# A planned order of some 3,600 steps, planned again with later transfers: fused block-sparse attention and a gated MLP on one core

## The chip, the core and the metric

The kernel runs on one core of a Trainium2 chip. Its work is spread over TensorE (PE, with its weight loads shown apart as PEld), VectorE (DVE), ScalarE (ACT), GpSimd (POOL) and the DMA queue that SyncE (SP) feeds; each of them carries out its own instructions in the order in which they were written and waits at semaphores for the others. The metric is the device time of one execution in microseconds (us), lower is better. Three runs of the kernel before took 992.58, 995.05 and 990.33 us; their median is 992.58 us.

## What is computed

The reference is attention with a block mask, followed by an MLP whose middle is `h * relu6(h + 3) / 6`:

```python
batch, n_heads, seq, head_dim = (4, 8, 768, 64)
scores = scale * np.matmul(q, k.transpose(0, 1, 3, 2))
...
scores = np.where(mask, scores, -1000000000.0)
scores = scores - np.max(scores, axis=-1, keepdims=True)
attn = np.exp(scores)
attn = attn / (np.sum(attn, axis=-1, keepdims=True) + 1e-09)
x = np.matmul(attn, v)          # then heads side by side: 3072 x 512
h = x @ w_in                    # 512 -> 2048
g = h * np.clip(h + 3.0, 0.0, 6.0) / 6.0
out = g @ w_out                 # 2048 -> 512
```

All inputs are float32. The mask works on blocks of 32 keys: neighbours, first and last block, and three sampled blocks in each row.

## The kernel before

**Two kinds of work, 64 pieces each.** A *unit* (`u0` to `u63`) is one head, one batch and half of the queries (384). A *step* (`m0` to `m63`) is one eighth of the MLP (two 128-wide chunks of the hidden layer) for one half batch. The MLP is computed with each fp32 number split into a high part and a low part, so a step has three products where one would do: high by high, high by low, low by high. The split of the two weight matrices is made by 32 pieces of *weight* work (`w0` to `w31`) in the first 210 us or so: load, four to five DVE and ACT passes, and a store of the low half to DRAM (`save`), from which steps load it again (`loadin_0`, `loadin_1`, `loadout_0`, `loadout_1`; tiles `wlo_in` and `wlo_out`, four buffers each). The high halves stay in SBUF (`win_hi`, `wout_hi`).

**A unit's steps.** `loadq`, `loadk`, `loadv` bring `qraw`, `kraw` and `vo` (one buffer of `qraw` and of `kraw`). `qh` and `kh` (ACT) and `ql` (DVE) make the tiles `QA` and `KA`; `kl` (POOL) and `qb` (ACT) make the low parts `kb` and `qb`. `m_0` to `m_2` (PE) compute scores whose block maxima `r_0` to `r_2` (DVE, tile `bm`) take; `fin_0`, `fin_1` give the row maximum `mneg`; `mt` carries it into a row of `qb` (from unit 10 on by a small DMA). `s_0` to `s_2` (PE) compute the scores again with the maximum and the mask added, `e_0` to `e_2` (ACT) the exponentials `pr`, `suma` to `sumc` (DVE) the sums, `av` (PE) the product with the values. `tt` (ACT) and `uu` (DVE) bring the product out of PSUM. For four units together `dm` (PE), `dc` (ACT), `rg` (four small DMAs), `rc` (DVE), `rs` and `rb` (DMAs by way of DRAM) make the reciprocal of the sums; `ux_0`, `ux_1`, `ux_2` (DVE, ACT, DVE) multiply by it and split the result into the pair `xhl`, which the steps read.

**A step's.** `h_00` to `h_11` (six matmuls each of 384 columns) fill one PSUM tile `big`; `ga` (ACT), `gb` (DVE), `gh` (ACT), `gl` (POOL) make `ghi` and `glo`; `o_00` to `o_21` (three matmuls each of 512 columns) add into `out0` to `out2`. The low halves of the weights are read by the third matmul of each three in `h` and by the second in `o`. Every eighth step ends with `oc` (DVE copies) and `od` (stores).

**What sets the order.** Nothing is scheduled at run time. The table `SCORE` (lines 41 to 299) lists some 3,600 steps in one order; `play` (line 858) goes through it and emits the instructions of each, and the wrapper `Ordered` (line 325) pins every instruction to that program order on its engine. The tile library adds the semaphores. The table was written by a planner from assumed durations and landing times. PSUM has two `big` tiles, one `av` tile and three `out` tiles. All work goes through the wrapper's line, so the profile names L333 nearly everywhere; tiles tell the steps apart.

Of the kernel before, what the change touches and what calls it, by code (L numbers as in the profile page):

```python
# [46 lines left out]
    bits_1; u2 qh; u0 e_1 av_1 e_2; u2 ql; w1 bits_2; u1 r_1 kl; w1 high low; u0 av_2; u1 m_2 r_2 fin_0 fin_1; u0 uc;
    u2 loadk kh m_0; w5 load; w3 size; u1 mt; u2 kl r_0; u3 loadk; u1 qm s_0 s_1; w3 bits_0; u2 m_1; w5 size bits_0;
    u1 e_0; u0 dw; w5 bits_1; u1 s_2; w3 bits_1; u1 e_1; w5 bits_2 high; u1 av_0; u2 loadv; u1 e_2; u2 qb; u3 loadq
    qh; u2 r_1 m_2; u1 av_1 av_2; u3 qb; w0 save; w5 low; u2 r_2 fin_0; w3 bits_2; u3 kh; u2 fin_1 mt; w3 high; u3 ql  # L50
    m_0 r_0; w4 load; u3 kl; w6 load; u2 qm s_0; w4 size; u3 m_1; u2 e_0; u1 uc; u2 s_1; u1 dw; w4 bits_0; u3 r_1; u2
    e_1 s_2; u3 m_2; w4 bits_1 bits_2; u4 loadq qh loadk; w6 size; u1 rg; u4 kh; u2 av_0; u3 r_2; u4 ql; w6 bits_0;
    u2 av_1 e_2; u3 fin_0; u4 qb; u3 fin_1; u1 rc; u4 m_0 r_0; u3 mt qm loadv; u2 av_2; w6 bits_1; w4 high low; u2
    uc; u3 s_0 e_0; u5 loadq; u2 dw; w6 bits_2 high; u4 m_1 r_1 kl; w3 low; u3 s_1 s_2; w7 load; u4 m_2 r_2; u5 qh ql
    loadk; u3 e_1; u1 rs; w8 load; u4 fin_0; u5 kh; w6 low; u6 loadq; u3 av_0; u4 fin_1; u3 av_1; u5 m_0 r_0; u4 mt;
    u3 e_2; w7 size; w8 size; u5 kl; w8 bits_0; u3 av_2; u4 qm s_0; w7 bits_0; u1 rb; w8 bits_1; u4 loadv; u5 m_1
    r_1; u4 s_1; u3 dw; u6 loadk; u4 e_0; w8 bits_2; u3 uc; w7 bits_1; u1 ux_0; u3 rg; u4 s_2 e_1; w10 load; u6 qh ql
    kh; u5 m_2 r_2; u4 e_2 av_0 av_1; u6 m_0; u3 rc; u4 av_2; u1 ux_1; u6 kl; u7 loadq; u5 qb; w8 high; w10 size; u7
    loadk; u5 loadv; w6 save; u5 fin_0 fin_1 mt; u6 r_0; w7 bits_2; u6 m_1; w10 bits_0; u6 r_1; u5 qm; u6 loadv; u4
    uc; w7 high low; w4 save; u5 s_0 s_1; u6 m_2; u5 e_0; u4 dw; u5 s_2 e_1 av_0 av_1; u1 ux_2; w10 bits_1; u6 r_2;  # L60
    w2 save; u7 qh ql; w9 load; u3 rs; u6 fin_0; w10 bits_2; u5 e_2; u6 fin_1; u7 kh m_0 r_0; u6 qb; w9 size; u6 mt;
    u7 kl; u6 qm; u5 av_2; u8 loadq; w8 low; w10 high low; u5 dw; w9 bits_0; u6 s_0 e_0; u7 m_1 r_1; m1 loadin_0; w9
    bits_1; u5 uc; u6 s_1 e_1; u3 rb ux_0; w9 bits_2; u6 s_2; w3 save; u8 loadk; u7 m_2; u8 qh ql kh; u6 av_0 av_1
    e_2; u5 rg rc; u7 r_2 fin_0; w11 load; w12 load; u8 kl; u3 ux_1 ux_2; w11 size; u7 fin_1; u6 av_2; w11 bits_0; w5
    save; w10 save; u8 m_0; u7 qb; u8 r_0; u7 mt; w9 high; u6 uc; w11 bits_1; u7 qm; w9 low; u7 s_0; u6 dw; u7 e_0;
    u8 m_1 r_1; u5 rs; w12 size bits_0; u7 s_1 e_1; w8 save; u7 s_2 loadv; u8 m_2; u9 loadk kh loadq; u7 av_0; u9 kl;
    u7 e_2; u9 qh; u7 av_1; m1 loadout_0; w7 save; u7 av_2; u5 rb; u8 qb; m0 loadout_1; u9 qb; w11 bits_2; w12
    bits_1; w14 load; u8 r_2 fin_0; u5 ux_0; u8 fin_1; u9 ql; w11 high low; u10 loadk; u5 ux_1; u8 mt qm; u9 m_0 m_1
    r_0; u7 dw uc; u10 loadq; w14 size; u8 s_0; u9 r_1; u8 e_0 s_1 s_2 e_1; w9 save; u10 kh kl; w12 bits_2 high; u10
    qh; m1 loadin_1; u8 loadv; m0 loadout_0; w14 bits_0 bits_1 bits_2; u9 m_2; u5 ux_2; u7 rg rc; u8 av_0; u9 r_2; u8  # L70
    av_1 e_2; u9 fin_0 fin_1 mt; w16 load size; u8 av_2; w14 high; u10 ql m_0; w16 bits_0 bits_1; u9 loadv; m1
    loadout_1; u9 qm; w18 load; u7 rs; u8 uc dw; u10 r_0; u9 s_0 e_0; w14 low; w16 bits_2; w18 size; u11 loadk; u9
    s_1 e_1; u10 qb; w11 save; u7 rb; w18 bits_0; u9 s_2 e_2 av_0; u11 kh; w18 bits_1 bits_2; w12 low; u10 m_1 r_1
    m_2 r_2; m0 loadin_1; u9 av_1; m0 loadin_0; w18 high; u7 ux_0; u10 fin_0; w16 high; u11 loadq; w13 load; w14
    save; u11 qh ql; u7 ux_1 ux_2; w1 save; w12 save; m0 h_00; w13 size bits_0 bits_1; w15 load size; w13 bits_2; m0
    h_10; w17 load; u12 loadq; m0 h_01; u9 av_2 dw; u11 qb; m0 h_11 ga; u11 kl loadv; w15 bits_0 bits_1; u10 fin_1
    mt; w15 bits_2; w16 low save; m1 h_00; m0 gb; m1 h_10 h_01 h_11; w18 low; u10 qm s_0; w13 high; u12 loadk; w19
    load; w15 high; m0 gh gl; w18 save; m2 loadin_0; w17 size; w13 low save; m0 o_00 o_10 o_20; m1 ga; u9 rg; u10
    loadv e_0; w17 bits_0; u9 uc; w15 low; u10 s_1; w19 size; w17 bits_1; m1 gb; u10 e_1 s_2; u12 kh; u10 e_2; m0
    o_01; w17 bits_2; w19 bits_0; u11 m_0; w22 load; w15 save; m2 loadin_1; u12 qh kl; m0 o_11 o_21; w19 bits_1  # L80
    bits_2; m1 gh; u11 r_0; w20 load; u11 m_1 m_2 r_1 r_2 fin_0; w22 size; w19 high; w20 size; u10 av_0; u12 ql; w17
    high; w19 low; u11 fin_1; w22 bits_0 bits_1; m1 gl; w22 bits_2; m2 h_00 h_10 h_01 h_11; u12 m_0; m2 ga; w20
    bits_0; m1 o_00 o_01; w17 low; w20 bits_1; u12 r_0; w22 high; u12 qb; m2 gb; m1 o_10; w19 save; u11 mt qm; m2 gh
    loadout_1; u12 m_1; m1 o_11; w20 bits_2; u12 m_2; m1 o_20; u12 r_1 r_2 fin_0; w21 load size bits_0 bits_1; w20
    high; u10 av_1; u12 fin_1; u11 s_0; w21 bits_2; u11 s_1; u13 loadk; u11 e_0; u13 loadq; w24 load; w22 low; m2
    loadout_0; w17 save; u11 e_1; m1 o_21; u11 s_2; w24 size; u13 qh; w21 high; u10 av_2 dw; m3 loadout_0; w24
    bits_0; m2 gl o_00 o_10; u12 mt; m3 loadin_1; u12 qm; w23 load; w22 save; u11 e_2; u12 s_0 s_1; m2 o_01; u10 uc;
    u9 rc; m3 loadout_1; m2 o_11; w24 bits_1 bits_2; u13 kh; u11 av_0; u12 e_0; w21 low; w23 size; w24 high; w20 low;
    u13 ql m_0; w21 save; u12 loadv; w23 bits_0 bits_1; w24 low; u13 r_0 kl; w26 load size; u9 rs; u12 e_1; m2 o_20;
    m3 loadin_0; w23 bits_2; u11 av_1; w23 high; m4 loadin_0; u9 rb; u13 m_1 m_2; u11 av_2; w26 bits_0; u13 r_1 r_2;  # L90
    w20 save; u14 loadq; u12 s_2; u11 dw; w26 bits_1 bits_2; u11 uc; u13 fin_0; w23 low; u9 ux_0; w26 high; m3 h_00
    h_01 h_10; u12 e_2; w24 save; u12 suma; u14 qh; w25 load; u14 loadk kh kl; m5 loadin_0; u14 qb; u13 qb fin_1; m3
    h_11; u14 ql m_0; w28 load; u14 r_0; m3 ga gb gh; u12 sumb; w28 size; u12 av; u14 m_1; m4 loadin_1; u11 rg; u13
    mt qm; u14 r_1; u13 s_0; m3 gl; u13 e_0; m2 o_21; u14 m_2; u15 loadk; m3 o_00; m4 loadout_0; u13 s_1; u11 rc; u14
    r_2; u13 s_2; u12 tt; w25 size; m3 o_01; u13 e_1 e_2; w25 bits_0 bits_1; m4 h_00 h_10; m5 loadin_1; u15 loadq;
    u13 loadv; m4 h_01; u15 qh; w26 low; w25 bits_2 high; u14 fin_0; u12 sumc; w25 low; u15 ql; m4 loadout_1; u15 kh
# [809 lines left out]
```

## Time and profile before

| | before |
|---|---|
| three runs, median | 992.58 us (990.33 to 995.05) |
| the profiled execution's own time | 991.15 us |
| its span, first to last instruction | 989.4 us |
| PE busy / weight loads busy | 947.2 us / 769.7 us |
| DVE, ACT, POOL busy | 620.6, 465.3, 247.4 us |
| DMA | 155 MB, 737 issues, all from SP |

The span is the length of the profiled execution between its first and its last instruction; 1.75 us of its own time lie outside. Matmul rows overlap: a 384-column matmul is listed with 338 ns, while the next one begins some 175 ns later. A stretch's own pace is therefore read from rows of many matmuls in the chain of waits (so many matmuls in so many us), and idle time from what stands in brackets behind a row: how long the engine stood still before it and what ended that.

### The profile page before, as it was taken

The page shows a single profiled execution, that of the slowest core. Times are in us where ns is not written, and L with a number is a line of the kernel's source. Part 1 is how long each engine was busy: PE and PEld are TensorE (multiplying, and loading weights), DVE is VectorE, ACT ScalarE, POOL GpSimd, SP SyncE. Part 2 cuts the span into 40 slices and gives each one's busy share as a digit, 9 for nine tenths or more (in the row PEclk, how much of TensorE's full clock was granted, in tenths as well). Part 3 has the DMA queues.
Part 4 walks back from the last instruction along what each step waited for, and adds up shares of the span by engine and source line. Part 5 has one row for each costly group of instructions (what it writes and reads, how often), then busy time and mean ns, then how long its engine had stood idle before and what let it go on. Part 6 is the DMA issues. An engine that isn't in the chain of part 4 may idle for free.

```text
span 989.4 us, 13166 instructions
## 1 busy us (share of the span) xinstructions
PE 947.2 (96%) x4756; PEld 769.7 (78%) x4756; DVE 620.6 (63%) x924; ACT 465.3 (47%) x712; POOL 247.4 (25%) x148
## 2 busy tenths in 40 slices
PE   5998999999999999999999999999999999999998
PEld 4665787877787788877877788897788778888997
DVE  6988887955757555487565576676655686543111
ACT  5888765543444344435454444354353544442211
POOL 3222222221313122223232322132322222222122
PEclk9999999999999999999999999999999999999999
DMA  5679876664254443544435446346434444353533
GB/s 179 194 227 272 264 266 218 200 196 136 86 171 133 155 155 118 155 144 132 149 124 163 127 128 206 104 128 185 146 108 152 148 139 132 115 157 99 163 107 106
DMA packets 103700, 155.47 MB, mean 157 GB/s; under 512 B 32819, under 2 KB 51891, under 8 KB 103636
## 3 DMA queue, kind: packets, MB, share of 16 engines
q1 hardware_dynamic: 103636, 154.64, 50.0%
q8 instruction: 37, 0.61, 0.3%
q14 instruction: 27, 0.22, 0.1%
HBM read 139.63 MB, written 14.78 MB: 156 GB/s over the span
## 4 chain that ended last, share of the span: by engine, by line
PE 71%; DMA 14%; DVE 7%; ACT 3%; SPq 3%; issue 2%; DVEq 0%; ACTq 0%
PE big L333 39%; PE out L333 21%; PE av L333 11%; SPq L333 3%; DMA kraw<-kT 3%; DMA qb<-mneg 2%; DVE bm L333 2%; DVE xhl L333 2%; DMA wout_lo<-xhl 2%; DMA rec<-rec 1%; DMA wraw<-w_out 1%; DMA wlo_in<-win_lo 1%; DMA win_lo<-xhl 1%; ACT pr L333 1%; DVE acc L333 1%
## 5 line engine op out<-in xcount | busy, mean ns | idle before, releaser
L333 PE MATMUL big<-xhl,win_hi 128*128 128x384 f32 x1024 | 263.3, 338 | 0.3 <-DVE bm L333 0.2
L333 DVE TENSOR_REDUCE bm<-big 128x24 f32<-128x768 f32 x168 | 158.4, 953 | 105.6 <-PE big L333 104.7
L333 POOL TENSOR_TENSOR glo<-g,ghi 128x768 fp32r<-128x768 f32 x64 | 120.6, 1885 | 389.4 <-ACT ghi L333 380.1
L333 ACT ACTIVATE pr<-big 128x768 f32<-128x768 f32 x192 | 152.8, 810 | 125.5 <-PE big L333 123.0
L333 POOL TENSOR_TENSOR kb<-kraw,KA 64x768 fp32r<-64x768 f32 x64 | 122.0, 1907 | 340.3 <-ACT KA L333 267.0
L333 PEld LDWEIGHTS big<-xhl,win_hi 128*128 128x128 f32 x1024 | 186.0, 188 | 10.6 <-issue 3.7
L333 PE MATMUL big<-xhl,wlo_in 128*128 128x384 f32 x512 | 173.2, 338 | 2.4 <-DMA wlo_in<-win_lo 2.4
L333 PE MATMUL av<-pr,vo 128*64 128x384 f32 (+1 forms) x768 | 164.7, 497 | 1.3 <-DVE uu L333 0.6
L333 PE MATMUL out<-wlo_out,ghi 128*128 128x512 f32 x384 | 151.4, 394 | 3.1 <-DMA wlo_out<-wout_lo 3.1
L333 PE MATMUL out<-wout_hi,glo 128*128 128x512 f32 x384 | 152.9, 398 | 0.3 <-POOL glo L333 0.3
L333 PE MATMUL out<-wout_hi,ghi 128*128 128x512 f32 x384 | 153.1, 399 | 0.0
L333 PE MATMUL big<-QA,KA 128*128 128x384 f32 x384 | 136.8, 356 | 2.8 <-DVE g L333 1.1
L333 PE MATMUL big<-qb,kb 97*128 97x384 f32 x384 | 133.6, 348 | 5.3 <-DMA qb<-mneg 2.5
L333 PEld LDWEIGHTS av<-pr,vo 128*64 128x64 f32 (+1 forms) x768 | 66.9, 147 | 67.6 <-issue 48.8
L333 ACT ACTIVATE g<-big,half_b 128x768 f32<-128x768 f32 x64 | 57.7, 902 | 126.1 <-PE big L333 111.7
L333 DVE SCALAR_TENSOR_TENSOR g<-g,big 128x768 f32<-128x768 f32 x64 | 60.8, 950 | 82.9 <-ACT g L333 82.6
L333 PE MATMUL big<-KA,QA 128*128 128x384 f32 x336 | 93.5, 369 | 16.9 <-ACT KA L333 11.3
L333 PEld LDWEIGHTS big<-KA,QA 128*128 128x128 f32 x336 | 75.0, 255 | 41.1 <-ACT KA L333 13.5
L333 PEld LDWEIGHTS big<-xhl,wlo_in 128*128 128x128 f32 x512 | 96.1, 188 | 3.1 <-DMA wlo_in<-win_lo 3.1
L333 PEld LDWEIGHTS big<-QA,KA 128*128 128x128 f32 x384 | 74.0, 193 | 17.8 <-issue 3.0
L333 ACT CAST ghi<-g 128x768 fp32r<-128x768 f32 x64 | 53.2, 832 | 71.0 <-PE out L333 44.7
L333 PEld LDWEIGHTS out<-wout_hi,glo 128*128 128x128 f32 x384 | 72.4, 188 | 18.1 <-POOL glo L333 0.7
(63 smaller groups left out, 937.4 us busy)
## 6 DMA issues: line engine op xcount, KB each, us to landing
wlo_in<-win_lo SPq DMA_DIRECT2D x126, 256.0 KB, 3.6
wlo_out<-wout_lo SPq DMA_DIRECT2D x126, 256.0 KB, 3.5
kraw<-kT SPq DMA_DIRECT2D x64, 384.0 KB, 3.7
qraw<-qT SPq DMA_DIRECT2D x64, 192.0 KB, 2.8
vo<-vP SPq DMA_DIRECT2D x64, 192.0 KB, 3.6
wraw<-w_in SPq DMA_DIRECT2D x16, 512.0 KB, 4.2
wraw<-w_out SPq DMA_DIRECT2D x16, 512.0 KB, 3.6
rec<-rec SPq DMA_DIRECT2D x64, 96.0 KB, 3.1
```

Of the source, the lines that this page charges most:

```text
L333: return lambda *a, **k: tc.keep_in_program_order(op(*a, **k))
```

## The change

Everything outside the table `SCORE` stays word for word. The table has the same steps, each once, in another order. The planner that wrote it was told later landing times for transfers and longer times for issuing them. Two lines of it, before and after:

```diff
-    u0 loadq qh; k0 samp; u0 loadk; k0 table; u0 ql kh m_0; k0 index; u0 m_1; k0 ind allow_0; w0 load size; k0 kb_0
...
-    o_00 loadout_1 o_01 o_10 o_11 oc_0 od_0 oc_1 od_1 o_20 o_21 oc_2 od_2"""
...
+    m_0 r_0; m41 o_10; m43 h_00; u53 m_1; u54 qh; m43 loadin_1 h_10; u53 r_1; u54 ql; m43 h_01; u52 suma; u54 m_0;
...
+    oc_2 od_2 od_1"""
```

**Place one, the DMA queue of SP around the load of step `m5`'s second output chunk.** `wout_lo11` is that chunk in DRAM, `wlo_out` the tile it lands in, `spread<-rec` the four small DMAs of unit 15's `rg`. Before:

```order
L333 DMA wlo_out_2016<-wout_lo10_100 128x512
L333 DMA spread_2044<-rec_2026 32x1x12 x4
L333 DMA vo0_119<-vP 128x384
L333 DMA wout_lo13_103<-xhl_1790 128x512
L333 DMA wlo_out_2084<-wout_lo11_101 128x512
L333 DMA wlo_in_2091<-win_lo3_77 128x512
L333 DMA rec15_2106<-spread_2044 128x12
```

And in the changed kernel:

```order
L333 DMA wout_lo12_102<-xhl_1650 128x512
L333 DMA win_lo15_89<-xhl_1867 128x512
L333 DMA wlo_out_1991<-wout_lo11_101 128x512
L333 DMA wlo_in_2013<-win_lo14_88 128x512
L333 DMA wraw_2016<-w_out 128x1024
L333 DMA wlo_in_2037<-win_lo15_89 128x512
L333 DMA wlo_in_2040<-win_lo0_74 128x512
L333 DMA kraw_2042<-kT 128x768
L333 DMA wlo_out_2044<-wout_lo12_102 128x512
L333 DMA spread_2048<-rec_2046 32x1x12 x4
```

The load of `wout_lo11` stood three rows behind the four small DMAs; now it stands seven rows ahead of them. On PE, `o_01` of `m5`, its first reader, stands 35 matmuls behind unit 15's `dm` before (24 of `h`, 8 of `s`, 3 of `o`) and 36 behind it now (24 of `h`, 4 of `s`, 2 of `m`, 6 of `o`); `dm` is what the four small DMAs wait for, by way of ACT.

**Place two, the same queue a little later, around the load of step `m9`'s first input chunk.** `win_lo2` is that chunk, `rec<-rec15` are the broadcasts (`rb`) of units 13 and 15, two DMAs each. Before:

```order
L333 DMA rec_2122<-rec15_2106 64x384 x2
L333 DMA qraw_2125<-qT 128x384
L333 DMA wlo_out_2139<-wout_lo13_103 128x512
L333 DMA wout_lo14_104<-xhl_2006 128x512
L333 DMA rec_2158<-rec15_2106 64x384 x2
L333 DMA kraw_2176<-kT 128x768
L333 DMA wlo_out_2178<-wout_lo14_104 128x512
L333 DMA wlo_in_2180<-win_lo2_76 128x512
L333 DMA wout_lo15_105<-xhl_1928 128x512
```

And in the changed kernel:

```order
L333 DMA vo1_120<-vP 128x384
L333 DMA wlo_in_2116<-win_lo3_77 128x512
L333 DMA rec15_2121<-spread_2048 128x12
L333 DMA wlo_out_2123<-wout_lo13_103 128x512
L333 DMA wout_lo14_104<-xhl_1852 128x512
L333 DMA wlo_in_2140<-win_lo2_76 128x512
L333 DMA rec_2146<-rec15_2121 64x384 x2
L333 DMA rec_2150<-rec15_2121 64x384 x2
L333 DMA wout_lo15_105<-xhl_2053 128x512
```

The load of `win_lo2` stood behind both broadcasts, a `kraw` load and the load of `wout_lo14`; now it stands ahead of all four. On PE its first reader, `h_00` of `m9`, stands 80 matmuls behind unit 15's `dm` before (36 of `h`, 30 of `o`, 8 of `s`, 6 of `m`) and 94 behind it now (48, 36, 4 and 6).

**Place three, PE near the end, around the last attention product.** `av<-pr` is unit 63's `av`, `big<-xhl` the first matmul of `m56 h_01`, which needs the results of units 60 to 63. Before, unit 63's `av` stands like this:

```order
L333 MATMUL av_8244<-pr_8123,vo1_120 64x384 x2
L333 MATMUL av_8244<-pr_8171,vo1_120 64x384 x2
L333 MATMUL av_8244<-pr_8205,vo1_120 64x384 x2
L333 MATMUL big_8253<-acc_7914,ones_116 32x384
L333 MATMUL big_8253<-acc_8058,ones_116 32x384
L333 MATMUL big_8253<-acc_8207,ones_116 32x384
L333 MATMUL big_8253<-acc_8242,ones_116 32x384
L333 MATMUL big_8209<-xhl_7503,win_hi_72 128x384 x2
L333 MATMUL big_8209<-xhl_7503,wlo_in_8151 128x384
```

and in the changed kernel like this:

```order
L333 MATMUL av_8397<-pr_8186,vo1_120 64x384 x2
L333 MATMUL av_8397<-pr_8213,vo1_120 64x384 x2
L333 MATMUL out0_7701<-wout_hi_73,ghi_8308 128x512
L333 MATMUL out0_7701<-wlo_out_8352,ghi_8308 128x512
L333 MATMUL out0_7701<-wout_hi_73,glo_8309 128x512
L333 MATMUL out1_7702<-wout_hi_73,ghi_8308 128x512
L333 MATMUL out1_7702<-wlo_out_8352,ghi_8308 128x512
L333 MATMUL out1_7702<-wout_hi_73,glo_8309 128x512
L333 MATMUL out2_7703<-wout_hi_73,ghi_8308 128x512
L333 MATMUL out2_7703<-wlo_out_8352,ghi_8308 128x512
L333 MATMUL out2_7703<-wout_hi_73,glo_8309 128x512
L333 MATMUL big_8318<-xhl_8372,win_hi_72 128x384 x2
```

Before, 42 matmuls of `h`, 36 of `o` and the four of `dm` stood between that `av` and `m56 h_01`; now nine of `o` do. The matmuls of `dm` came right behind `av`; now they stand 54 of `h` and 45 of `o` ahead of it.

## Rows read from the trace of the kernel before

**Rows 1.** The busy time of each engine, its share of the span and its number of instructions (the page's first part).

```profile
PE 947.2 (96%) x4756; PEld 769.7 (78%) x4756; DVE 620.6 (63%) x924; ACT 465.3 (47%) x712; POOL 247.4 (25%) x148
```

**Rows 2.** The chain that ended last, in order of time: start in us, duration in us, what, how many. Pieces in which PE ran without a gap, one for each kind of matmul.

```profile
439.99 2.80 PE big L333 x16
442.79 2.09 PE av L333 x12
...
960.46 4.19 PE out L333 x18
964.64 4.22 PE big L333 x24
```

**Rows 3.** Who PE waited for between 200 and 975 us: engine, tile, line, releaser; us in total, times, longest wait. Some smaller rows are left out.

```profile
PE out L333 <- DMA wlo_out<-wout_lo: 3.1, 2, 2.4
PE big L333 <- DVE QA L333: 2.6, 3, 1.1
PE big L333 <- DMA wlo_in<-win_lo: 2.4, 2, 1.6
PE big L333 <- ACT KA L333: 2.2, 4, 0.9
PE big L333 <- DVE bm L333: 2.1, 4, 1.1
PE big L333 <- DMA qb<-mneg: 1.8, 4, 0.6
```

**Rows 4.** The same view between 0 and 200 us, its first row.

```profile
PE big L333 <- ACT KA L333: 9.0, 2, 6.6
```

**Rows 5.** Instructions of PE in order of time around 209 us: start, duration, operation; in brackets the idle time before it and what ended that.

```profile
208.69 0.40 PE L333 MATMUL out<-wout_hi,ghi 128*128 128x512 f32 x1
211.53 0.50 PE L333 MATMUL out<-wlo_out,ghi 128*128 128x512 f32 x1 [2.44 <-DMA wlo_out<-wout_lo]
```

**Rows 6.** The DMA issues of SP in order of time around 210 us: start, how long SP was at it, what.

```profile
203.32 2.49 SPq L333 DMA_DIRECT2D spread<-rec  x4
...
206.95 0.43 SPq L333 DMA_DIRECT2D wlo_out<-wout_lo  x1
...
219.03 0.43 SPq L333 DMA_DIRECT2D wlo_in<-win_lo  x1
```

**Rows 7.** Two stretches of 3 us: the stretch, its length, busy us of PE, PEld, DVE, ACT and POOL with the number of instructions, the clock granted to TensorE as a share of full speed, the DMA engines' busy share, GB/s.

```profile
159.00:162.00 3.00, 3.00 (x11) 1.15 (x12) 2.69 (x3) 1.55 (x4) 1.12 (x1) 0.55 0.34 78
213.00:216.00 3.00, 3.00 (x9) 2.32 (x8) 2.82 (x4) 0.00 (x0) 0.00 (x0) 0.50 0.33 102
```

**Rows 8.** Instructions of PE around 224 us, columns as in rows 5.

```profile
224.55 0.44 PE L333 MATMUL big<-xhl,wlo_in 128*128 128x384 f32 x1 [1.64 <-DMA wlo_in<-win_lo]
```

**Rows 9.** Instructions of PE around 158 us, columns as in rows 5.

```profile
158.23 1.01 PE L333 MATMUL big<-KA,QA 128*128 128x384 f32 x2 [2.45 <-ACT KA L333]
```

**Rows 10.** The chain that ended last, columns as in rows 2: transfers that were waited for in the first 230 us, from issue to landing.

```profile
62.62 5.20 DMA wraw<-w_out
73.91 6.56 DMA wout_lo<-xhl
104.12 5.61 DMA wraw<-w_out
134.28 5.24 DMA wout_lo<-xhl
151.05 6.28 DMA kraw<-kT
...
219.03 5.48 DMA wlo_in<-win_lo
```

**Rows 11.** The same chain between 238 and 287 us: what ended two waits of PE for KA and QA.

```profile
266.48 2.15 DVE QA L333
...
276.73 5.48 DMA kraw<-kT
```

**Rows 12.** Groups of equal instructions: line, engine, operation, output<-input, shapes, count; busy us in all, mean ns of one; idle time before them and what ended it.

```profile
L333 ACT COPY tmp<-av 64x384 f32<-64x384 f32 x52 | 24.7, 475 | 77.3 <-PE av L333 76.7
L333 DVE TENSOR_TENSOR uu<-av,tmp 64x384 f32<-64x384 f32 x52 | 28.8, 553 | 37.0 <-ACT tmp L333 36.4
L333 DVE TENSOR_TENSOR uu<-uu,rec 128x384 f32<-128x384 f32 x32 | 20.8, 660 | 11.5 <-DMA rec<-rec 11.5
L333 ACT CAST xhl<-uu 128x384 fp32r<-128x384 f32 x32 | 16.1, 509 | 20.1 <-DVE uu L333 20.1
L333 DVE TENSOR_TENSOR xhl<-uu,xhl 128x384 fp32r<-128x384 f32 x32 | 20.2, 639 | 6.7 <-ACT xhl L333 6.6
```

**Rows 13.** Stretches of 25 us, columns as in rows 7.

```profile
75.00:100.00 25.00, 21.32 (x82) 14.73 (x82) 20.93 (x38) 20.10 (x35) 5.49 (x3) 0.93 0.90 270
100.00:125.00 25.00, 23.18 (x111) 19.44 (x110) 20.04 (x34) 18.13 (x30) 6.32 (x4) 1.00 0.83 271
...
200.00:225.00 25.00, 20.92 (x102) 16.84 (x99) 15.16 (x25) 11.16 (x19) 6.03 (x3) 0.93 0.59 186
```

**Rows 14.** DMA issues by kind: output<-input, queue, operation, count, KB each, median us from issue to landing.

```profile
wlo_out<-wout_lo SPq DMA_DIRECT2D x126, 256.0 KB, 3.5
kraw<-kT SPq DMA_DIRECT2D x64, 384.0 KB, 3.7
...
wraw<-w_in SPq DMA_DIRECT2D x16, 512.0 KB, 4.2
```

More of the change, by code (lines that the diff above doesn't have):

```diff
@@ L47 @@
[L47 to L96, printed above, removed]
@@ new lines @@
+    w10 save; u7 loadv; u6 s_1 s_2 e_1; u5 rg; u6 e_2; w12 load; u7 r_1; u8 qh; w8 low; u3 ux_0; u8 ql kh; u6 av_0;
+    u5 rc; u7 m_2 r_2; u6 av_1; w7 save; w11 size; w9 high; u7 fin_0 fin_1; u6 av_2; u7 qb; u3 ux_1; w6 save; u8 m_0;
+    w11 bits_0; u9 loadq; u6 dw; u7 mt qm s_0; w12 size; u7 e_0; u8 kl; w1 save; u8 r_0; w11 bits_1; u6 uc; u3 ux_2;
+    w11 bits_2; u7 s_1; w12 bits_0; u8 m_1; w9 low; u8 r_1; u5 rs; w8 save; w12 bits_1; u7 s_2; u9 loadk; u7 av_0
+    e_1; m1 loadout_1; u8 m_2 r_2; w11 high; u8 fin_0 loadv fin_1; u9 kh; m1 loadin_0; u7 e_2 av_1; u5 rb; w14 load;
@@ new lines @@
+    u7 av_2; u8 qb; u9 qh kl qb; u8 mt qm; u9 ql; u5 ux_0; u9 m_0 m_1 r_0 r_1; u7 dw uc; w14 size; u10 loadk loadq;
+    u8 s_0 e_0; w12 bits_2; u8 s_1 e_1; u9 loadv; u7 rg; w11 low; w16 load; u8 s_2; w11 save; w14 bits_0 bits_1; u9
+    m_2; u5 ux_1; u7 rc rs; u8 e_2; w14 bits_2; w12 high; u10 qh; u9 r_2 fin_0; u10 kh; w14 high; u8 av_0 av_1; w18
+    load; u10 ql m_0; u9 fin_1 mt qm; w16 size; u10 r_0; u8 av_2; u7 rb; u8 dw; w14 low; u9 s_0 e_0 s_1 s_2; w18
+    size; u10 kl; u8 uc; u11 loadk; w12 low; w9 save; u11 loadq; u9 e_1; w16 bits_0; u5 ux_2; m0 loadin_0; u9 av_0
@@ new lines @@
+    e_2; w16 bits_1; m1 loadin_1; w18 bits_0; w16 bits_2; w18 bits_1; u7 ux_0; m0 loadin_1; u10 m_1; w12 save; u11
+    kh; w18 bits_2; u10 m_2 r_1; u11 kl; u10 r_2; w16 high; u10 fin_0 fin_1; u9 av_1; w14 save; w13 load; w15 load;
+    m0 h_00 h_10; u10 qb mt; w18 high low; u7 ux_1 ux_2; m0 h_01; w16 low; u11 qh; w16 save; w13 size bits_0 bits_1
+    bits_2; u10 qm; m0 loadout_1 loadout_0 h_11; m2 loadin_1; w17 load; w15 size; m0 ga; w15 bits_0 bits_1; m0 gb gh;
+    m1 h_00 h_01; w15 bits_2 high; w13 high; u11 ql; w18 save; w13 low; w15 low; w19 load; m1 h_10 h_11; m0 gl; u10
@@ new lines @@
+    w29 bits_0; u16 fin_1; w30 bits_0; m5 loadout_0; u14 av; u15 s_0 s_1 e_0 e_1; w30 bits_1; w25 low; u16 kl; m5 gl;
+    m4 o_20; w29 bits_1; u16 qb mt qm; u17 loadq; m6 h_00; w30 bits_2; u16 loadv; u15 suma; u14 tt uu; u11 rb; u15
+    s_2 e_2; w30 high low; u15 sumb; m6 h_01 h_10 h_11; m8 loadin_1; u15 sumc; u11 ux_0; w25 save; u16 s_0; m4 o_01
+    o_11 o_21; u17 qh; m6 ga gb gh; w30 save; m5 loadout_1; u9 ux_0 ux_1 ux_2; u16 s_1 e_0 e_1; u15 av; m7 loadin_0;
+    w29 bits_2; w31 load; u15 dm; u17 ql; m7 h_00 h_01 loadin_1; m6 gl; m8 loadin_0; u17 loadk; m6 loadout_0; u15 dc
@@ new lines @@
+    rg; w31 size; w29 high; u16 s_2; u11 ux_1; u18 loadq; w31 bits_0; u16 e_2; u17 kh kl; m7 h_10 h_11; m5 o_00; w31
+    bits_1 bits_2; u19 loadv; u17 m_0; m5 o_10 o_01 o_11 o_20; w29 low; m5 o_21; u15 rc; w31 high low; m7 ga gb; m9
+    loadin_1; m7 gh; u17 r_0; u15 rs; m6 loadout_1; w29 save; u11 ux_2; m8 h_00 h_10; m9 loadin_0; u17 m_1 r_1; u13
+    rb ux_0; u15 rb; w31 save; m6 o_00 o_10; u15 tt uu ux_0; u17 qb; u13 ux_1 ux_2; m7 loadout_0; u15 ux_1 ux_2; u17
+    m_2; u18 loadk kh; u17 r_2 fin_0; u18 qh ql; m7 gl; m6 o_01 o_11 o_20 o_21; m8 loadout_1; m7 loadout_1; m8
@@ new lines @@
+    loadout_0; u63 rs; m55 ga gb gh gl; m57 loadin_0; u61 rb ux_0 ux_1 ux_2; m57 h_00 h_10; m54 o_00 o_10 o_20; u63
+    av tt uu; m55 loadout_0; u63 rb ux_0; m54 o_01 o_11 o_21; u63 ux_1 ux_2; m56 h_01 h_11 ga gb gh gl; m55
+    loadout_1; m57 h_01; m59 loadin_0; m57 h_11; m59 loadin_1; m58 loadin_1; m56 loadout_1; m55 o_00 o_01 o_10; m58
+    loadin_0; m59 h_00 h_01; m55 oc_0; m59 h_10 h_11; m55 o_20 o_11 o_21; m61 loadin_0; m57 ga gb; m56 loadout_0; m58
+    h_00; m57 gh; m61 loadin_1; m57 gl; m47 od_2; m58 h_10 h_01; m57 loadout_1 loadout_0; m55 od_0 oc_1 oc_2; m60
```

434 lines of the change are left out of this document (227 added, 207 removed).

## The prediction, made before the changed kernel ran

> **What bounds the kernel now.** I read the busy shares first: PE is busy for 947.2 us of 989.4, and no other engine comes near [rows 1]. Then the chain of waits for PE's own pace, since matmul rows overlap: 16 matmuls of `big` in 2.80 us and 24 in 4.22 us are 0.175 us each, 18 of `out` in 4.19 us are 0.233 us each, 12 of `av` in 2.09 us are 0.174 us each [rows 2]. A step (24 of the first, 18 of the second) is 8.41 us, the matmuls of a unit (18 of the first, 12 of `av`) 3.15 + 2.09 = 5.24 us; 64 of both are 874 us. The first twelve units' wider `av`, `dm` and the start add to that; still some 70 to 100 us of the span are PE standing still or running at a lower pace, more than the 42 us that the busy row leaves.
>
> The Trainium skill ("Perfetto Trace Analysis", Identifying the Most-Contended Engine) says the same of that row: matmul busy time is no good measure of how close PE is to its limit, and weight loads' busy share is a better one. Here that share is 78% [rows 1]; by it up to 22% would be open, by the paces above some 10%. The sum below needs neither.
>
> Then the waits of PE, and here the kernel has two parts. From 200 us on PE waits rarely and mostly for transfers: 3.1 us for the low output weights, 2.4 for the low input weights, 1.8 for the maximum row `qb`, and 2.2 and 2.6 for `KA` and `QA`, the tiles that ACT and DVE make out of `kraw` and `qraw` [rows 3]. Before that DVE and ACT are busy for 20 of 25 us and the DMA engines for 0.83 to 0.90 [rows 13]; transfers that were waited for there took 5.2 to 6.6 us, against medians of 3.5 to 4.2 over the whole kernel [rows 10, 14]. A plan made with short landing times is right in the second part except where the queue is blocked, and wrong in the first.
>
> **The change part by part.** No instruction is added or removed, so PE's 874 us of work stay, and so do DVE's and ACT's. What can change is waiting.
>
> *Place one: −4.1 us.* PE stood still for 2.44 us at 209 us for a `wlo_out` [rows 5]. SP issued that load at 206.95 us, behind unit 15's four small DMAs, which alone held SP for 2.49 us from 203.32 on [rows 6]; it landed 4.5 us later. In the new order it stands seven rows ahead of those four. Its reader stands 30 matmuls of 0.175 and 6 of 0.233 us behind unit 15's `dm`, 6.65 us; the four DMAs wait for `dm`, so the load, ahead of them, has at least that and needs 4.5. The 2.44 us go. With them goes what followed: from 213 to 216 us, right after this pause, the granted clock was 0.50, so the chip was at 1.2 instead of 2.4 GHz, and 9 matmuls stood in 3 us [rows 7] where the pace of 0.233 us makes 12.9. That is a loss of about 1.3 us in those 3; since the window of 200 to 225 us has a mean clock of 0.93 [rows 13], the low stretch is 25 x 0.07 / 0.5 = 3.5 us and costs 1.7 us. Together 4.1.
>
> *Place two: −1.6 us.* PE waited 1.64 us at 224.5 us for a `wlo_in` [rows 8], issued at 219.03 [rows 6] and landed after 5.48 [rows 10], behind two pairs of broadcasts and two other loads. Now it stands ahead of all of these, and 14 more matmuls stand between `dm` and its reader, 2.5 to 3 us. The wait goes.
>
> *The other loads of low weights: −1.5 us.* The two rows hold four waits, 3.1 + 2.4 = 5.5 us [rows 3]; without the two above 1.4 to 1.5 remain. Bounds: 0 if other loads take their place, −1.5 if all go. I take all, since the new table places these loads with longer landings throughout.
>
> *`KA` and `QA` after 200 us: −2.4 us.* Together 4.8 us in seven waits [rows 3]. Some were transfers (`kraw` 5.48 us at 276.73), one was a DVE instruction of 2.15 us [rows 11] that no order of transfers touches. So between 0 and −4.8; I take half.
>
> *`qb`: −0.6 us* of 1.8 [rows 3]. This small DMA hangs on a chain of DVE instructions behind the third score matmul, and the orders keep about the same number of matmuls between; between +1 and −1.8.
>
> *DVE's `bm`, 2.1 us [rows 3]: 0.* It waits for DVE, not for transfers; between −2 and +2.
>
> *The first 200 us: 0, between −6 and +6.* PE waits 9.0 us for `KA` here, 6.6 of them for the very first load [rows 4], and 2.45 us for unit 14's [rows 9], behind a `kraw` of 6.28 us [rows 10], again followed by a clock of 0.55 [rows 7]. In the new table some 2.4 us of matmuls lie between the place of that `kraw` load in the queue and its reader, where 2.1 lay before, so I expect this wait to stay. The orders of the weight work, and the share of DVE's and ACT's work that stands ahead of a given point of PE's, are nearly the same in both tables. DVE has 20 us of work in 25 there [rows 13], and a better place for a transfer gives back at most what DVE leaves.
>
> *Place three, the added wait: +0.6 us.* Behind unit 63's `av` stood 78 matmuls of steps before `m56 h_01`; now nine of `o` do, and the first three of `h_01` read the other pair: 9 x 0.233 + 3 x 0.175 = 2.6 us. In that time the product must go through `tt`, `uu`, `ux_0`, `ux_1`, `ux_2`: 0.475 + 0.553 + 0.660 + 0.509 + 0.639 = 2.84 us [rows 12], with five hand-overs some 3.2. So 0.6 us late if ACT and DVE are free just then; nothing else is ready for PE, as all of its queue stands behind this matmul. Bounds: −0.4 and +3 if one other instruction of each engine comes between. The reciprocal, which `dm` starts, has far more room than before, 99 matmuls.
>
> *The end: +0.4 us.* The last `od` in the queue is now that of `out1`, behind the one of `out2` that waits for the last copy: one more issue of 0.43 us [rows 6], between 0 and +0.5.
>
> Sum: −4.1 − 1.6 − 1.5 − 2.4 − 0.6 + 0.6 + 0.4 = −9.2 us. The profiled execution took 991.15 us, 1.4 below the median of the three runs; against it 982.0, against the median 983.4. I forecast 983.5 us.
>
> **The rivals.**
>
> *The waits only move (about 988.5 us).* With PE earlier at a place, the next slow thing is reached earlier too, a `bm` on DVE or a `kraw` that waits for POOL. For it: PE's waits after 200 us are many and small, none but the two above over 1.1 us [rows 3]. Against it: in the window of 200 to 225 us DVE is busy for 15 of 25 us and ACT for 11 [rows 13], so what comes next is not late by itself. Then only place one with its clock stays, −4.1: 991.15 − 4.1 = 987.0, 988.5 on the median.
>
> *The first part pays for it (about 999 us, slower).* Transfers brought forward fall into the stretch of 50 to 175 us, where the DMA engines are at 0.83 to 0.90 [rows 13] and one more transfer in flight lengthens the others. `kraw` has one buffer and its landing leads straight to PE. Twelve units (3 to 14) load there; if each `kraw` lands 1.3 us later, half of the way from the median 3.7 to 6.28 [rows 10, 14], PE loses 15.6 us, and −9.2 + 15.6 = +6.4: 999. It decides from 14 / 12 = 1.2 us for each unit on, where the loss is 5 us over the gain. For it: a landing of 6.56 us at 74 us [rows 10]. Against it: the number of issues ahead of a given point of PE's work hardly differs between the tables in this stretch, so the traffic is the same.
>
> A rule of the Trainium skill ("DMA: Bandwidth & Descriptors", Latency and other measured facts) speaks for this rival: access to HBM takes 0.2 us on average and 2 us at high load, and that is the larger part of a transfer's fixed cost. By it, an estimate, a `kraw` under full load could be 1.8 us later, 12 x 1.8 = 21.6 us. The landings above agree with its direction; no row shows the split.
>
> *The new table is no earlier where it matters.* Several loads of the second chunk of output weights stand directly ahead of their reader in the table. SP runs ahead of the table where nothing blocks it, so this would show as waits for `wlo_out` at other places, of up to 2.4 us each as in place one. Two of them would take the gain down to the first rival's.
>
> **How the numbers follow.** The forecast 0.6, with its own range 978 to 987.5; the waits only move 0.27 (with the third rival in it), 985 to 993; slower 0.13, from 993 to 1001. The whole range is 976.5 to 993: it takes in −6 of the first part at its lower end and the first rival's upper end. Within 0.5% of 992.58 is 987.6 to 997.5, about what a measurement tells from no change. From the forecast 0.57 lie below it and 0.03 inside; of the first rival 0.05 below and 0.22 inside; of the slower one 0.04 inside and 0.09 above. Faster 0.62, same 0.29, slower 0.09.
>
> **What would show it.** Right: no wait of PE for `wlo_out` or `wlo_in` over 0.5 us after 200 us; a granted clock of 1.00 in all stretches from 200 us to the end but the last; waits for `KA` and `QA` after 200 us below 3 us; a wait of 0.3 to 1.5 us for `xhl` at `m56 h_01`. Wrong: a wait for `KA` or for ACT and DVE in the first 200 us longer in sum than before, or a second low stretch of the clock at a new place, each worth 1.7 us on top of its wait.

## The result, and the profile after

The changed kernel took 967.02 us (median; 964.97 to 968.04), the kernel before in the same session 991.83 us: a ratio of 0.9743 (0.9713 to 0.9773). It is faster, by 25 us where 9 were forecast, and lies below the range.

The busy time of each engine and the shares of the chain that ended last, of the changed kernel:

```profile
PE 937.4 (97%) x4756; PEld 768.7 (80%) x4756; DVE 618.7 (64%) x924; ACT 464.1 (48%) x712; POOL 250.3 (26%) x148
...
PE 87%; DVE 6%; DMA 3%; ACT 2%; issue 1%; SPq 0%; POOL 0%; DVEq 0%; ACTq 0%
```

The work is that of [rows 1] within 2%. The chain has changed: of the kernel before its row reads

```profile
PE 71%; DMA 14%; DVE 7%; ACT 3%; SPq 3%; issue 2%; DVEq 0%; ACTq 0%
```

so the transfers and the queue, which made up 17% of the chain, make up 3% of it now.

Who PE waited for in the changed kernel between 200 and 975 us, columns as in [rows 3], all its rows:

```profile
PE big L333 <- DVE QA L333: 2.5, 1, 2.5
PE big L333 <- DVE bm L333: 0.9, 1, 0.9
PE big L333 <- DVE xhl L333: 0.4, 1, 0.4
PE av L333 <- DVE uu L333: 0.4, 1, 0.4
PE big L333 <- DMA qb<-mneg: 0.3, 1, 0.3
```

No wait for `wlo_out` or `wlo_in` is left, none for `KA`, and one for `QA` that is new (below). The 0.4 us for `xhl` stand at 568.5 us and have nothing to do with place three. There, behind unit 63's `av`, no wait is long enough for a row:

```profile
894.58 0.56 DVE L333 TENSOR_TENSOR xhl<-uu,xhl 128x384 fp32r<-128x384 f32 x1 [0.58 <-ACT xhl L333]
...
894.94 0.70 PE L333 MATMUL big<-xhl,win_hi 128*128 128x384 f32 x2
895.47 0.34 PE L333 MATMUL big<-xhl,wlo_in 128*128 128x384 f32 x1
```

The two matmuls around DVE's last write take 0.53 us (894.94 to 895.47) where the pace makes 0.35. So place three costs some 0.2 us; 0.6 were forecast. Between 0 and 200 us, the first rows:

```profile
PE big L333 <- ACT KA L333: 6.5, 1, 6.5
PE big L333 <- DVE mneg L333: 6.2, 2, 4.7
```

Against [rows 4] one of the two waits for `KA` is gone, unit 14's; the very first stays. The two for `mneg` lie at the start, at 17.2 and 28.8 us, and are longer than before (2.6 us in all). The clock in the stretches that were low in [rows 7] and [rows 13], columns as there:

```profile
200.00:225.00 25.00, 25.00 (x129) 23.01 (x128) 15.94 (x23) 10.51 (x16) 7.33 (x4) 1.00 0.56 181
...
62.00:65.00 3.00, 3.00 (x12) 2.07 (x10) 2.38 (x6) 1.27 (x3) 0.00 (x0) 0.67 0.69 189
158.00:161.00 3.00, 3.00 (x17) 1.67 (x18) 3.00 (x5) 2.44 (x5) 0.00 (x0) 1.00 0.84 278
213.00:216.00 3.00, 3.00 (x16) 2.64 (x16) 2.24 (x5) 0.95 (x2) 0.00 (x0) 1.00 0.77 271
```

PE is busy for all of 200 to 225 us (20.92 before), and from 200 us on the granted clock is 1.00 until the last stretch, as forecast. One low stretch is new: 0.67 between 62 and 65 us, behind a wait of PE of 1.8 us for `QA` at 61.6.

**Where the time went.** Waits alone don't add up to 25 us, since PE also loses pieces too short for a row. So I place both traces on one scale: each matmul in its order gets its pace (0.175 us for `big` and `av`, 0.233 for `out` [rows 2], about 0.32 for the wide `av` of the first twelve units, from its pitch), the sum so far is PE's own work, and the start of a matmul minus the work ahead of it is what was lost until then. How the few other matmuls are priced shifts the entries by some us in both kernels alike; the differences between the kernels stay. The boundary at 120 us lies just ahead of unit 14's wait. In us, one profiled execution each; "front" is the first 200 us of work, "back" the rest:

| | lost by 120 us of work | from 120 to 200 | back |
|---|---|---|---|
| before | 34.6 | 14.0 | 37.3 |
| after | 34.2 | 2.2 | 25.7 |

By this scale half of the gain lies around the boundary between the two parts, in 80 us of work, and half is spread over the 700 us behind it.

Of the 11.8 us saved between 120 and 200, 5.7 are the forecast prices of places one and two, and some 4.1 are unit 14's wait for `KA` (2.45 us [rows 9]) and the low stretch behind it (1.7). How that wait went can be read from SP. Its issues in the kernel before, columns as in [rows 6]:

```profile
148.89 0.54 SPq L333 DMA_DIRECT2D win_lo<-xhl  x1
149.53 0.37 SPq L333 DMA_DIRECT2D qraw<-qT  x1
149.99 0.45 SPq L333 DMA_DIRECT2D win_lo<-xhl  x1
150.53 0.43 SPq L333 DMA_DIRECT2D wraw<-w_out  x1
151.05 0.41 SPq L333 DMA_DIRECT2D kraw<-kT  x1
```

and in the changed kernel:

```profile
144.27 0.33 SPq L333 DMA_DIRECT2D wraw<-w_in  x1
145.97 0.33 SPq L333 DMA_DIRECT2D kraw<-kT  x1
150.27 0.33 SPq L333 DMA_DIRECT2D win_lo<-xhl  x1
```

The buffer of `kraw` comes free when POOL's `kb` of the unit before ends. That row, before and then after:

```profile
143.91 1.83 POOL L333 TENSOR_TENSOR kb<-kraw,KA 64x768 fp32r<-64x768 f32 x1 [8.37 <-ACT KA L333]
...
143.74 2.21 POOL L333 TENSOR_TENSOR kb<-kraw,KA 64x768 fp32r<-64x768 f32 x1 [3.10 <-ACT KA L333]
```

Before, the buffer was free at 145.74 us, but other issues stood ahead and the load went out at 151.05, 5.3 us later; PE wanted `KA` at 155.78 (158.23 less the wait of 2.45), 4.7 us behind the issue. Now the buffer is free at 145.95, the load goes out at once, and PE reads `KA` 7.8 us behind the issue without a wait:

```profile
153.76 0.81 PE L333 MATMUL big<-KA,QA 128*128 128x384 f32 x2
```

So the load has 3.1 us more. Before, it landed after 6.28 us [rows 10]; whether it lands sooner now the trace does not tell, as nothing waits for it.

### The profile page after: what moved, and what is told of

The parts are those of the page before. It is cut to its first block, busy times and chain, and to the rows that moved or that the text cites. A ratio compares the mean times of both kernels' runs of the same rounds, so it can differ in the third digit from the quotient of the medians.

```text
span 966.3 us, 13209 instructions
## 1 busy us (share of the span) xinstructions
PE 937.4 (97%) x4756; PEld 768.7 (80%) x4756; DVE 618.7 (64%) x924; ACT 464.1 (48%) x712; POOL 250.3 (26%) x148
## 4 chain that ended last, share of the span: by engine, by line
PE 87%; DVE 6%; DMA 3%; ACT 2%; issue 1%; SPq 0%; POOL 0%; DVEq 0%; ACTq 0%
PE big L333 47%; PE out L333 27%; PE av L333 13%; DVE xhl L333 2%; DVE bm L333 2%; DMA wraw<-w_in 1%; DVE acc L333 1%; DMA wraw<-w_out 1%; ACT pr L333 0%; DVE QA L333 0%; DMA spread<-rec 0%; DMA qb<-mneg 0%; ACT xhl L333 0%; SPq L333 0%; POOL kb L333 0%
## 5 line engine op out<-in xcount | busy, mean ns | idle before, releaser
L333 PE MATMUL big<-KA,QA 128*128 128x384 f32 x336 | 91.2, 360 | 11.4 <-ACT KA L333 6.5
```

What stands on the lines that cost most here:

```text
L333: return lambda *a, **k: tc.keep_in_program_order(op(*a, **k))
```

## The experiments

The first theory was that of the prediction: places add up, each worth its wait and the clock behind it. Its rivals: the waits only move, and the gain comes of the orders of all engines together. Each edit is one of the table; nothing else is touched.

**Front and back apart.**

```diff
-    all steps, old order
+    steps ahead of 200 us of PE's work, new order; the others, old order
```

> The new order up to the point where PE has done 200 us of its work (the 248.6th us of the profile before), then the old order for everything left. Theory 'each part by itself': the gain is local, so this gives what the two traces differ by at that point, 12.2 us: 979.6 us, ratio 0.988. Rival 'front alone': the gain is made in the crowded first part and only carried along: 967 to 970 us. Rival 'back alone': under 3 us of gain, 989 us or more.

```diff
-    all steps, old order
+    steps ahead of 200 us of PE's work, old order; the others, new order
```

> The old order up to the same point, then the new one. Theory 'each part by itself': the rest of the difference, 11.6 us: 980.2 us, ratio 0.988. Rival 'front alone': 988 to 992 us. Rival 'back alone': 967 to 971 us. If the two gains of this kernel and the last add up to 24 us within 3, the parts do not depend on each other.

Measured: 978.88 us, 0.9827 (0.9785 to 0.9868), and 989.1 us, 0.9932 (0.9902 to 0.9961). The two gains, 1.7% and 0.7%, make the whole of 2.6% up to 0.2%. So front and back are separate gains, and by these ratios the front has the larger. The pair of traces in the table above gives them as nearly equal, because the profiled execution of before was one whose old front loses little (48.6 us; 55.1 in the second run here, 52.1 to 57.3 in others below).

**The queue alone, the engines alone.**

```diff
-    transfers of the old order (all but the loads of w)
+    the same in the new order's sequence, the other steps in the old one
```

> Old order of all work on PE, DVE, ACT and POOL; the transfers (loads of q, k, v and of low weight halves, stores of low halves, the row of maxima, the reciprocal's small DMAs; the loads of raw weights not) stand in SP's queue at the point of PE's work where the new table has them, or as soon after it as their data and buffers allow. Theory 'queue': the order of transfers makes the gain: 967 to 975 us. Rival 'compute': the order on the engines makes it: 985 us or more, and slower than before if the two orders need each other.

```diff
-    transfers of the new order (all but the loads of w)
+    the same in the old order's sequence, the other steps in the new one
```

> The reverse: the new order on PE, DVE, ACT and POOL, the same transfers at the point of PE's work where the old table has them, or as soon after as data and buffers allow. Theory 'queue': the gain is gone, 985 us or more. Rival 'compute': 967 to 975 us.

Measured: 1052.76 us, 1.0573 (1.0524 to 1.0622), and 1090.59 us, 1.0943 (1.0886 to 1.1001). Both mixtures are slower than either kernel. They are orders that nobody planned, and some transfers had to be shifted where the two sequences would have blocked each other. So they show that the old order of one side does not go with the new order of the other; which side makes the gain they cannot tell.

**Single places.** In the old order, place one alone; then unit 14's `kraw` alone, ahead of the burst; then both and place two:

```diff
+    m5 loadout_1
     u15 rg
...
-    m5 loadout_1
```

> The old order with one step moved: the load of m5's second output chunk stands ahead of unit 15's four small DMAs instead of behind them (and the value load and the store that followed). Theory 'a pause costs itself and the low clock behind it': the wait of 2.44 us and the clock of 0.50 after it both go, -4.1 us, ratio 0.996. Rival 'the waits only move': the pause turns up again at the next load, 0 to -1.5 us.

```diff
+    u14 loadk
     w20 save
...
-    u14 loadk
```

> The old order with one step moved: unit 14's kraw load stands five rows further ahead in SP's queue, ahead of the stores of w20 and w24, unit 14's q load and the 512 KB load of w25. Its buffer is free 5.3 us before it was issued (POOL's kb ended at 145.74, the issue was at 151.05). Theory 'what stands ahead in the queue': issue at about 149, no w25 in front of it, so the wait of 2.45 us shrinks to 0.5 or less and the low clock behind it goes: -3.5 us, ratio 0.9965. Rival, my prediction's view that the crowded engines set this wait: it lands no earlier, 0 to -1 us.

```diff
+    u14 loadk
     w20 save
...
+    m5 loadout_1
     u15 rg
...
+    m9 loadin_0
     u13 rb
```

> The old order with three loads moved: the two above and the load of m9's first input chunk, which now stands ahead of both pairs of broadcasts. Theory 'places add up': -4.1 - 3.5 - 1.6 = -9.2 us, ratio 0.991, and no granted clock under 1.00 between 130 and 960 us. If it reaches that, three loads of 737 make a third of the whole gain. Rival 'the waits only move': -4 us or less.

Measured: 0.9997 (0.9965 to 1.0029), 0.998 (0.9944 to 1.0015) and 0.9951 (0.9929 to 0.9974). Unit 14's wait for `KA` falls from 2.45 to 1.1 us in the second run, and 2.2 us for `qb` and 3.2 for `wlo_in` follow; its interval holds both its forecast (0.9965) and no change. Forecast for place one were 4.1 us, which its interval just leaves out. In its run PE's wait for `wlo_out` is gone, and this stands at the next load, in PE's rows and in the windows of 3 us behind it:

```profile
225.71 0.44 PE L326 MATMUL big<-xhl,wlo_in 128*128 128x384 f32 x1 [3.49 <-DMA wlo_in<-win_lo]
...
225.00:228.00 3.00, 2.29 (x8) 2.00 (x9) 0.00 (x0) 0.00 (x0) 0.00 (x0) 0.76 0.60 193
228.00:231.00 3.00, 3.00 (x12) 2.71 (x12) 0.00 (x0) 0.00 (x0) 0.00 (x0) 0.68 0.42 134
```

The wait of [rows 8] is longer by 1.85 us, and the low stretch of [rows 7] has moved with it. Three places together bring 0.5%, half of the 1.0% that their waits and low stretches were worth in the trace (2.44 + 1.64 + 2.45 us, and twice 1.7). That is more than the rival's 4 us and less than the theory's 9.2.

**Place one undone in the new order.**

```diff
-    m5 loadout_1
...
     u19 loadv
+    m5 loadout_1
     u17 m_0
```

> The new order with one step moved back: the load of m5's second output chunk stands behind unit 15's four small DMAs, the q load and the value load, as it stood in the old one. It would be issued at about 202.6 us and land 4.5 later, 1.9 us after its reader is due at 205.18. Theory 'a pause costs itself and the low clock behind it': +1.9 to +3.6 us, 969 to 971 us, ratio against before 0.977 to 0.978. Rival 'the new order has slack here that the old one had not': 967 us, ratio 0.974.

Measured: 967.87 us, 0.9733 (0.9692 to 0.9775): no loss clear of noise, but the interval holds the rival's 0.974 and the lower end of the theory's loss (0.977). In the trace PE waits 1.01 us at that load, and the clock stays at 1.00 behind it. So of the 4.1 us that the same place was priced at in the old order the new one pays some 1 us, and alone in the old order the move brought nothing clear of noise: the price of a place depends on the order around it.

**Fifteen short leads in the old order's back.** Twelve loads of low weights (not nine, as the text says), two `kraw` and one `vo` move up; then the same with the three places:

```diff
+    u34 loadk
     u31 rg
...
-    u34 loadk
```

> The old order; fifteen transfers behind 200 us of PE's work (nine loads of low weights' second chunk or first chunk, four of them output weights waited for closely, two kraw, one vo) are moved two or four rows up in the queue, those that by the traces' median landing times had less than 1.5 us to spare ahead of their first reader. Theory 'short leads' (the back part's 11.6 us are the sum of such places): the waits for wlo_in and wlo_out behind 250 us (0.8 and 0.6 us) go, and some 2 us of those for KA and QA, so that the part behind 200 us of work loses 32 to 33 us instead of 37.3; ratio 0.995 to 0.996. Theory 'waits only move': the part loses 36 to 38 us as before, ratio 0.999 to 1.001. Theory 'margin everywhere': as in the new order, 26 us, ratio 0.988.

> The run before with the three moves around unit 14 and steps 5 and 9 as well (those alone gave 0.9951). If places add up once enough of them are mended: 0.990 to 0.991. If each mended place is lost again at the next: 0.995 to 0.998.

Measured: 1.0007 (0.9984 to 1.003) and 0.993 (0.9904 to 0.9956). The second lies between its two forecasts: on top of the fifteen, the three places are worth some 8 us, more than the 5 that they are worth without them and not far from the 9.2 of their prices. In the first PE's waits for `wlo_in` and `wlo_out` behind 240 us are gone, as meant, and the back loses 38.8 us all the same. The move shown above tells why. SP, DVE and PE in that run around 453 us:

```profile
451.55 0.33 SPq L327 DMA_DIRECT2D kraw<-kT  x1
451.94 2.48 SPq L327 DMA_DIRECT2D spread<-rec  x4
```

```profile
450.14 0.56 DVE L327 TENSOR_TENSOR uu<-av,tmp 64x384 f32<-64x384 f32 x1 [1.21 <-ACT tmp L327]
455.58 0.23 DVE L327 RECIPROCAL spread<-spread 128x12 f32<-128x12 f32 x1 [4.88 <-DMA spread<-rec]
455.84 0.95 DVE L327 SCALAR_TENSOR_TENSOR g<-g,big 128x768 f32<-128x768 f32 x1
```

```profile
456.85 0.44 PE L327 MATMUL big<-QA,KA 128*128 128x384 f32 x1 [2.47 <-DVE g L327]
```

and SP's own wait ahead of that `kraw`, from the queue's view of 440 to 455 us:

```profile
SPq L327 <- POOL kb L327: 5.9, 1, 5.9
```

In the kernel before the same reciprocal stood for 1.98 us:

```profile
450.12 0.23 DVE L333 RECIPROCAL spread<-spread 128x12 f32<-128x12 f32 x1 [1.98 <-DMA spread<-rec]
```

Read from the top: the load, now ahead of the four small DMAs, waits 5.9 us in SP's queue for its only buffer, which `kl` on POOL frees; the four small DMAs wait behind it; DVE stands 4.88 us at `rc` for what they bring; `g` stands behind `rc`; and PE waits 2.47 us for `g`. PE's row names `g`, not a transfer. A cure for a short lead of `kraw` has become a wait for the middle of the MLP, three queues on.

**The helpers moved out of the way.** In the second of those two orders, sixteen such steps of DVE and ACT go behind work that would have fitted:

```diff
-    u31 rc
     m23 gb
     u32 suma
...
     u32 sumb
+    u31 rc
```

> The order of the run with fifteen loads and three places mended (0.993), and in it sixteen steps of DVE and ACT that stood waiting for a transfer in that run's trace (rc, ux_0, kh, qh, a copy of the output) are moved behind those later steps of the same engine that would have fitted into the time they stood; the queue's order stays. In that trace DVE stands 4.88 us at 450 us for unit 31's spread, with g and two bm behind it, and PE waits 2.47 us for g. Theory 'an engine that stands for a transfer holds what is queued behind it': this wait for g goes, and part of those for bm, QA and qb (3.9, 2.6, 2.5 and 3.1 us behind 240 us in all), 3 to 6 us, ratio 0.987 to 0.990. Rival 'the waits only move again': 0.992 to 0.995, with the wait at 450 us gone and others in its place.

Measured: 994.23 us, 0.9982 (0.9955 to 1.0009). The order is some 5 us slower than the one that it mends (0.993), which neither theory forecast. The wait for `g` is gone; PE waits 4.4 us for `qb`, 3.1 for `QA`, 1.9 for `pr` and 1.8 for `bm` there. By the scale above the back loses 40.3 us here and some 43 in the order before the edit, but that trace is of its slowest execution (995.89 us, with a median of 988.34), so the two traces cannot tell where the 5 us lie. The chain through DVE is seen in the trace of the run before; that taking such steps out of the way helps is not borne out.

**Less lead in the new order.**

```diff
-    u30 loadk
...
+    u30 loadk
     u30 kh
```

and so for 178 loads.

> The new order; behind 200 us of work 178 loads (kraw, qraw, low weights) are moved down in the table until some 6.5 us of matmuls lie between them and their first reader, or as near to that as their buffers let them; the median lead falls from 13.8 to 11.0 us for wlo_in, from 15.1 to 12.4 for wlo_out, from 12.5 to 11.5 for kraw. Only four loads have less than their median landing time. Theory 'only the shortest leads count': 2 to 4 us lost at those four, 969 to 971 us, ratio 0.976 to 0.979. Theory 'the mean lead counts': the back part loses as much as in the old order, 11 us, 978 us, 0.986. If leads don't matter at all: 967, 0.974.

Measured: 982.28 us, 0.9862 (0.9832 to 0.9893): the back loses 40.2 us instead of 25.7, and the time is that of the theory "the mean lead counts". The trace does not bear that theory out as it stands, though: some 7 of the 14.5 us are lost at one load, and the rest at a few others. That load, rows in order of time on SP, ACT and PE, and the windows behind it:

```profile
392.51 0.38 SPq L326 DMA_DIRECT2D kraw<-kT  x1
...
396.93 0.83 ACT L326 CAST KA<-kraw 128x768 fp32r<-128x768 f32 x1 [2.39 <-DMA kraw<-kT]
...
398.08 1.49 ACT L326 ACTIVATE pr<-big 128x768 f32<-128x768 f32 x2
...
398.93 0.69 PE L326 MATMUL big<-QA,KA 128*128 128x384 f32 x1 [4.67 <-ACT pr L326]
```

```profile
398.00:401.00 3.00, 2.07 (x6) 2.07 (x7) 0.00 (x0) 1.96 (x4) 1.70 (x1) 0.50 0.17 20
401.00:404.00 3.00, 3.00 (x11) 3.00 (x11) 0.00 (x0) 1.63 (x3) 1.77 (x1) 0.53 0.74 261
```

ACT stands at this `kraw`'s cast until 4.4 us after its issue; the exponentials `pr` stand behind the cast, and PE waits 4.67 us for them, not for `KA`, with the clock at half behind that. So at this place the lead that counted was the one to the first instruction on *any* engine that reads the transfer, and its price was what stood behind that instruction. Whether short leads of this kind explain the rest of the loss, or the mean lead does, this run leaves open.

**One collision taken out.** The one long wait of the changed kernel, 2.5 us at 685.8 us, has another cause. POOL and DVE there:

```profile
680.31 2.13 POOL L333 TENSOR_TENSOR kb<-kraw,KA 64x768 fp32r<-64x768 f32 x1 [3.92 <-ACT KA L333]
680.65 1.89 DVE L333 TENSOR_TENSOR bm<-bm,mq 128x72 f32<-128x72 f32 x1
682.39 1.83 POOL L333 TENSOR_TENSOR glo<-g,ghi 128x768 fp32r<-128x768 f32 x1
682.46 2.58 DVE L333 TENSOR_TENSOR acc<-acc,pr 128x768 f32<-128x768 f32 x1
685.07 0.56 DVE L333 SCALAR_TENSOR_TENSOR QA<-qraw,QA 64x384 fp32r<-64x384 f32 x1
685.77 0.66 PE L333 MATMUL big<-KA,QA 128*128 128x384 f32 x2 [2.51 <-DVE QA L333]
```

The two DVE instructions that begin beside one of POOL end 0.10 and 0.82 us behind its end (680.31 + 2.13 and 682.39 + 1.83), as if most of their own 0.23 and 0.95 us had been done only then. `ql` (the `QA` row) stands behind both. The edit moves it ahead of them:

```diff
-    u48 suma
...
     u52 loadk
+    u52 qh
+    u52 ql
+    u48 suma
     u51 fin_0
-    u52 qh
     u48 sumb
-    u52 ql
```

> The new order with unit 52's ql moved ahead of three other DVE steps (suma and sumb of unit 48, fin_0 of unit 51). In the new order's trace PE waits 2.5 us for QA at 685.8 us, since two DVE instructions ahead of it, of 0.23 and 0.95 us elsewhere, took 1.89 and 2.58 us beside two of POOL. Theory 'DVE is held while POOL works': ql runs ahead of POOL's first, the 2.5 us go, 964 to 965 us, ratio 0.971 to 0.972. Rival 'the next thing is as late' (the sums or the maximum, now behind POOL): the wait turns up for pr or qb, 967 us, 0.974.

Measured: 964.6 us (961.46 to 965.55), 0.9685 (0.9656 to 0.9714). The changed kernel, in another session, had 967.02 us and 0.9743 (0.9713 to 0.9773): a gain of 2.4 us by the medians, more by the ratios, with intervals that just touch. Its rows at the same place:

```profile
678.44 0.56 DVE L325 SCALAR_TENSOR_TENSOR QA<-qraw,QA 64x384 fp32r<-64x384 f32 x1
679.00 1.83 POOL L325 TENSOR_TENSOR kb<-kraw,KA 64x768 fp32r<-64x768 f32 x1 [4.05 <-ACT KA L325]
679.01 2.69 DVE L325 TENSOR_TENSOR acc<-pr 128x768 f32<-128x768 f32 x1
...
682.66 0.69 PE L325 MATMUL big<-KA,QA 128*128 128x384 f32 x2 [0.87 <-ACT pr L325]
```

`acc` is now the one that is held, and 0.87 us of the wait come back by way of `pr`, so some 1.6 us are gained at this place. What the time fell by beyond that is not the edit's as far as the traces show; the low stretch of the changed kernel at 62 us, for one, is not in this execution.

## Why the prediction was right and wrong

Right: the direction; that PE bounds and keeps its work; that the waits of places one and two go [rows 5, 8] and the low stretch behind the first with them [rows 7]; that the clock stays at 1.00 from 200 us to the last stretch; the rival "the first part pays for it" did not come.

Wrong, in order of size:

- *"The first 200 us: 0 … so I expect this wait to stay."* This term and places one and two cover the same stretch of work, and between 120 and 200 us of it 11.8 us were saved where −5.7 stood in the sum; by the ratio of its own run the front gave 17 us. Unit 14's wait for `KA` went (2.45 us and a low stretch of 1.7). The step that failed is the lead of its `kraw` load: 2.1 us of matmuls against 2.4, so no change. The tables do not give these figures: between `u14 loadk` and the first matmul of `u14 m_0` stand 6 matmuls of `h` before (1.05 us), and now 12 of `h`, 4 of `s`, 3 of `o` and 4 of the wide `av` (some 4.8 us). By the traces the lead from issue to need grew from 4.7 to 7.8 us. What else makes up the 17 us is open.
- *"DVE's `bm`: 0. It waits for DVE, not for transfers"*, and *"`KA` and `QA`: I take half"*, *"`qb`: −0.6"*. Of 2.1, 4.8 and 1.8 us in [rows 3] 0.9, 2.5 and 0.3 are left, and the 2.5 are one collision with POOL. The back saved 11.6 us by the traces (0.7%, some 7 us, by the ratio of its own run) where these terms, the other low weights, place three and the end made −3.5. The step that failed is reading the name in a wait row as its cause. DVE and ACT stand at transfers themselves, 46 us in 25 pieces behind 240 us before, 29 us in 16 after, and what stands behind them appears in PE's rows as `g` or `pr`. The runs show this chain twice, link by link. That it makes up the whole of the back's gain is not shown, and the sum of those waits does not set the loss: with less lead they are 35 us in 24 pieces, and the back loses 40.2 us, more than the 37.3 of the old order. How the 11.6 us divide between these chains and loads that PE reads itself stays open.
- *Place one: −4.1 us*, as a price of its own. Alone it is worth 0 ± 3 us in the old order, and some 1 us of wait in the new one. "The waits only move" was the rival for the whole change, and it is wrong there; place one alone bears it out, unit 14's load alone can't tell, and the three together lie between it and the sum of their prices. (The 1.3 us in that term do not follow from 9 matmuls in place of 12.9, which make 0.9; its price used the 1.7 from the clock.)
- *Place three: +0.6 us.* It cost some 0.2, and the wait for `xhl` that was named as a sign did not appear.

The old order's executions ran from 987.75 to 1003.23 us over all sessions, those of the new order and its two near relatives (the undone place and the moved `ql`) from 961.46 to 970.67, none of the three over more than some 5 us. That thin margins cause the wider spread is not shown: the old order ran many times more often, and the order with less lead, too, spread over 5.2 us only. The old order's front lost 48.6 us in the one execution that I had a trace of, and 52 to 57 in four others, two of them with one load moved, which a single profile could not show.
